# Where four small sets of products stand: openings, maxima and stores in a gated attention and MLP kernel

## The chip, the cores and the metric

The kernel runs on one core of one Trainium2 chip. The metric is the device time of one execution in microseconds (us). TensorE (PE in the profile, its weight loads PEld), VectorE (DVE), ScalarE (ACT), GpSimd (POOL) and SyncE (SP) run side by side; each works through its own instructions in the order in which the program issues them, and semaphores hold an instruction until the data that it needs are there.

## The reference

For a sequence of 2048 tokens of width 448, all in float32, the output is `g * a + (1 - g) * b`, where `g` is a sigmoid of a weighted sum of the token.

- `a` is attention: 16 heads of width 28 have their own queries and share one key and one value head; `softmax(q k / sqrt(28)) v`, then an output projection `wo`.
- `b` is a mixer: layernorm, `w1`, gelu, the four quarters of the channels shifted by +1, -1, +2 and -2 tokens, `w2`, added to x to give `x1`; then layernorm, `w3` (448 to 1792), gelu, `w4`, added to `x1`.

## The kernel before, in words

Most products are made in two parts for precision: an operand is split into a high part and the low rest (tiles ending in `h` and `l`), and three products take the place of one. Names of tiles in the profile come from the program, buffer numbers left out.

The order of every engine's instructions is the order of the program text (`manual_schedule`). There are three stages.

**Stage 1** makes queries, keys and values and the token mixing. It begins with 16 products of zeros on TensorE (L97 and L98), which need no loaded data. `first_queries` (L319) then makes the queries of token block 0 from the raw first chunk (L324) and the split chunks (L328). There are 16 query blocks `u`, four groups of heads (`g`) for each of four token blocks (`b`); `stage_q(u)` (L331) makes one with eleven products and `q_out` (L313) copies it out of PSUM and stores it to DRAM from ScalarE's queue (L317). The rows of keys and values ride in the same blocks; `stage_kv(b)` (L341) reads them back on SyncE's queue (L345, L348), and on the same queue come the first weights of stage 2 (L605). `ln1_send(b)` (L375) transposes the inverse standard deviations of token block b on TensorE, copies them on ScalarE and writes them to DRAM on SyncE; `ln1_read(b)` (L383) reads them back spread over the partitions (L386), for `stage_w1(b)`, whose VectorE step multiplies by them (L453). `split_w_high` runs on ScalarE and `split_w_low` on VectorE; `ln1_tile(b, t)` takes the statistics of one token tile on VectorE.

**Stage 2** is the MLP: for each of four token blocks a loop over 14 feature tiles f, `w3_part` (products L136 to L140, two gelus on ScalarE, a difference on VectorE) and, two tiles behind, `w4_part` for four token tiles (products L693 to L695). In the third and fourth token block `fill()` (L669) puts a job between the token tiles: four jobs make the score maxima of query block 0, one token tile each, and a fifth (`max_end`) puts them in place.

**What the maxima are.** So that exponentials don't overflow, a stand-in for the largest score of each query is taken over 16 keys only. `max_products` (L207) makes 16 small bf16 products for a query block, four for each token tile, one in each of four column tiles of the array; `max_reduce` (L215) reduces them on VectorE; `max_end` (L244) negates, splits and transposes the maxima and stores them on SyncE into spare rows of the query tile `qh`.

**Stage 3** is the attention: 128 cycles `c`, eight for each query block `u` (`u, i = divmod(c, 8)`). PSUM's eight banks are four `singles` and two `pairs`. A cycle handles two tiles of keys:

1. the first scores (24 products, L205) go into two singles `s0`, `s1` and into `pairs[0]`; ScalarE makes exponentials of the singles and VectorE copies the pair out (L929), so that the pair is soon free again;
2. the second scores go into the other two singles and `pairs[1]`; ScalarE makes their exponentials, and then those of the copied pair;
3. the values of the cycle before (L883) go into the bank of `s0` for the first half of the queries, and into that of `s1` for the second; `values_end` adds each to the output on VectorE (L805);
4. jobs, products of the output projection for the query block before (L831) with their add on VectorE (L847), stand between.

In the next cycle the singles change places: the second scores go where this cycle's `s0` and `s1` were. At `i == MAX_AT` (2), for the first 15 query blocks, the maxima of the next block are made as well: one job goes into `pairs[0]` between the two halves of the values, and the maxima's products go into the second half of `s0` behind them. In cycles without maxima the job goes into the second half of `s0`, and at `i == 2` of the last query block there are both jobs.

Of the kernel before, what the change touches and what calls it, by code (L numbers as in the profile page):

```python
# [42 lines left out]
def gated_mix_kernel(  # L43
# [50 lines left out]
        return psA.tile([P, 512], F32, tag="mx", bufs=1, name=name)  # L94

    wps = misc_tile("warm_ps")
    for _ in range(16):  # L97
        nc.tensor.matmul(wps[:, 0:256], warm[:, 0:P], warm, start=True, stop=True)  # L98

    def split_w_chunk(raw, wh, wl, c, cols=slice(None)):  # L100
# [9 lines left out]
    def split_w_high(raw, wh, wl):  # L110
        nc.scalar.copy(wh[:, 0:3, :], raw[:, 0:3, :])
        nc.gpsimd.memset(f32(wh)[64:128, 3, :], 0.0)
        nc.scalar.copy(wh[0:64, 3, :], raw[0:64, 3, :])
        nc.scalar.copy(wl[64:128, 3, :], raw[64:128, 3, :])

    def split_w_low(raw, wh, wl):
        for c in range(3):
            nc.vector.tensor_tensor(wl[:, c, :], raw[:, c, :], f32(wh)[:, c, :], ALU.subtract)
        nc.vector.tensor_tensor(wl[0:64, 3, :], raw[0:64, 3, :], f32(wh)[0:64, 3, :], ALU.subtract)
# [87 lines left out]
    def max_products(u, ts, ps):  # L207
        for i, t in enumerate(ts):
            for c in range(4):
                m = t * P + 32 * c  # L210
                q = f32(qh_of[u])[:, m:m + 32].bitcast(BF16).rearrange("p (m e) -> p m e", e=2)[:, :, 1]
                nc.tensor.matmul(ps[32 * c:32 * c + 32, i * 4 * MK:(i + 1) * 4 * MK], q, khd,
                                 start=True, stop=True, tile_position=(0, 32 * c))

    def max_reduce(u, ts, ps):  # L215
        if u not in mx_of:
            mx_of[u] = late.tile([P, 4, 4], F32, tag="mr", bufs=2, name=f"mr_{u}")
        n = len(ts)
        nc.vector.reduce_max(mx_of[u][:, :, ts[0]:ts[0] + n].rearrange("p j t -> p t j"),
                             ps[:, 0:n * 4 * MK].rearrange("p (t j k) -> p t j k", t=n, j=4), axis=AX.X)  # L220

    def max_part(u, ts, ps):
        max_products(u, ts, ps)
        max_reduce(u, ts, ps)
# [19 lines left out]
    def max_end(u):  # L244
        mr = mx_of.pop(u).rearrange("p j t -> p (j t)")
        mc = late.tile([P, 32], F32R, tag="mc", bufs=2, name=f"mc_{u}")
        nc.vector.tensor_scalar(mc[:, 0:16], mr, -1.0, None, op0=ALU.mult)
        nc.vector.scalar_tensor_tensor(mc[:, 16:32], mr, -1.0, f32(mc)[:, 0:16],
                                       op0=ALU.mult, op1=ALU.subtract)
        mrow = late.tile([P, 32], F32, tag="mrow", bufs=2, name=f"mrow_{u}")  # L250
        nc.vector.transpose(mrow, f32(mc))
        for k in range(2):
            rows = f32(qh_of[u])[DH + k:P:32, :].rearrange("j (t p q) -> p j t q", p=4, q=32)
            for p in range(4):
                nc.sync.dma_start(rows[p], mrow[32 * p + 16 * k:32 * p + 16 * k + 16, :])
# [4 lines left out]
    with tc.tile_pool(name="s1b", bufs=1) as s1b, \  # L260
# [52 lines left out]
        def q_out(u, ps):  # L313
            b, g = divmod(u, NG)
            qf = s1.tile([P, 512], F32, tag="qf", bufs=4, name=f"qf_{u}")
            nc.scalar.copy(qf, ps)
            nc.scalar.dma_start(qd[g, :, 512 * b:512 * b + 512], qf)  # L317

        def first_queries():  # L319
            ps = [mm1(f"q_{g}") for g in range(NG)]  # L320
# [10 lines left out]
        def stage_q(u, tile_of=mm1):  # L331
            b, g = divmod(u, NG)
            ps = tile_of(f"q_{u}")
            w = slice(g * P, (g + 1) * P)
            proj(ps, wqh[:, :, w], wql[:, :, w], *xact[b])
            q_out(u, ps)
# [31 lines left out]
        def ln1_tile(b, t):  # L368
            if t == 0:
                rs1_of[b] = stats_tiles(s1, b)  # L370
            stats_tile(s1, b, t, rs1_of[b][0])
            if t == 3:
                stats_end(*rs1_of[b])

        def ln1_send(b):  # L375
            ps = misc_tile(f"rsT_{b}")[0:4, 0:P]
            nc.tensor.transpose(ps, rs1_of.pop(b)[1], ident)
            rT = s1.tile([4, P], F32, tag="rT", bufs=2, name=f"rT_{b}")
            nc.scalar.copy(rT, ps)
            rb_of[b] = dram.tile([4, P], F32, tag="rsd", bufs=2, name=f"rsd_{b}")  # L380
            nc.sync.dma_start(rb_of[b], rT)
# [128 lines left out]
        centre_w1()  # L510
        stage_q(7)
        stage_q(8)
        ln1_send(0)
        ln1_read(0)
        split_w_high(w1raw, w1h, w1l)
        for t in range(4):
            ln1_tile(1, t)
        split_w_low(w1raw, w1h, w1l)
        stage_q(9)
        load_x(3)  # L520
        stage_q(10)
        load_x1(3)
# [137 lines left out]
    with tc.tile_pool(name="s2", bufs=1, reuse_waits="tile") as s2, \  # L660
# [2 lines left out]
            for n in range(n0, n1):  # L663
                nc.gpsimd.tensor_scalar(x1[:, n, :], x1[:, n, :], gi[:, n:n + 1], None, op0=ALU.mult)

        fills = [lambda t=t: max_part(0, (t,), (max_tile if t % 2 else misc_tile)(f"m_0_{t}")) for t in range(4)]
        fills += [lambda: max_end(0)]

        def fill():  # L669
            if fills:  # L670
# [85 lines left out]
    with tc.tile_pool(name="s3", bufs=1, reuse_waits="tile") as s3, \  # L756
# [38 lines left out]
        def values_end(u, pv, qs=slice(0, 512)):  # L795
            if u not in o_of:
                o_of[u] = s3.tile([P, 512], F32, tag="o", bufs=2, name=f"o_{u}")
                fresh.add(u)
            o = o_of[u][:, qs]
            if u in fresh:  # L800
                nc.vector.tensor_copy(o, pv)
                if qs.stop == 512:
                    fresh.remove(u)
            else:
                nc.vector.tensor_add(o, o, pv)  # L805
# [88 lines left out]
        def job_products(ps, n):  # L894
            adds = []
            for _ in range(min(n, len(jobs))):
                products, add, args, cols = jobs.pop(0)
                part = ps[:, 0:D // 2] if n == 1 else ps[:, cols]
                products(*args, part, cols)
                adds.append((add, args, part, cols))  # L900
            return adds
# [11 lines left out]
        for c in range(NC):  # L913
            u, i = divmod(c, NT // 2)
            k = 2 * c
            s0, s1, s2, s3_ = singles if c % 2 == 0 else singles[2:] + singles[:2]
            pa = score_tiles(u, 2 * i, s0, s1, pairs[0])
            with tc.block() if c in HINTS else nullcontext():
                if c in HINTS:
                    tc.mark_branch_hint_location("redo", "LikelyTaken", HINTS[c])  # L920
                exps(pa, left, s0.unsqueeze(1))
            exps(pa, right, s1.unsqueeze(1))
            if i == 2 and u == 0:
                q_begin(1)
            if i == 3 and u == 0:
                q_low(1)
                q_fetch(2)
            if c < NC - 1:
                nc.vector.tensor_copy(pa[:, both], pairs[0])  # L929
            else:  # L930
                exps(pa, both, pairs[0])
            if i == 4 and later:
                later.pop(0)()
            if i == 1 and sums:
                norms.append(recip(*sums.pop()))
            if i == 3 and norms:
                w = norms[0][0]
                norm(*norms.pop())
            if i == 5 and u + 2 < NU:
                q_begin(u + 2)  # L940
            if i == 6 and u + 2 < NU:
                q_low(u + 2)
                q_fetch(u + 3)
            pb = score_tiles(u, 2 * i + 1, s2, s3_, pairs[1])
            exps(pb, left, s2.unsqueeze(1))
            exps(pb, right, s3_.unsqueeze(1))
            exps(pb, both, pairs[1])
            if c < NC - 1:
                exps(pa, both)
            if u and i == (3 if u == NU - 1 else 4):  # L950
                jobs += [(wo_products, wo_add, (u - 1, t), cols) for t in range(4) for cols in halves]
            if c == 0:
                run_jobs(s0, 2)
                run_jobs(s1, 2)
                continue
            v = (c - 1) // (NT // 2)
            at_max = i == MAX_AT and u + 1 < NU
            q0, q1 = slice(0, 256), slice(256, 512)
            values((k - 2, k - 1), s0[:, q0], q0)
            values_end(v, s0[:, q0], q0)  # L960
            if i == MAX_AT:
                run_jobs(pairs[0][:, 0], 1)
            values((k - 2, k - 1), s1[:, q0], q1)
            if at_max:
                max_products(u + 1, range(4), s0[:, q1])
                values_end(v, s1[:, q0], q1)
                max_reduce(u + 1, range(4), s0[:, q1])
                later.append(lambda u=u: max_end(u + 1))
            else:
                adds = job_products(s0[:, q1], 1)  # L970
                values_end(v, s1[:, q0], q1)
                job_adds(adds)
            if i == 0 and v < NU - 1:
                sums.append(sums_begin(v))
        assert not sums and not norms and not later and len(jobs) == 3
# [143 lines left out]
```

## Time and profile before

| | us |
|---|---|
| median of 3 runs | 928.12 |
| the runs | 927.07, 928.12, 928.72 |
| the profiled execution, its own time | 929.3 |
| its span | 927.4 |

The span runs from the first to the last instruction that the profile shows. In a row of a timeline stand the start and the length in us, the engine, the line of the kernel, the operation, and the tiles as `out<-in` with their shapes; `x16` merges neighbours of one kind, and the length then runs from the first start to the last end; in brackets stand the engine's idle time before it and who ended it. A busy length of a matmul includes its drain, so neighbours overlap, and the distance between starts tells the pace. In a row of waits stand the sum in us, the number of waits and the longest. "issue" means that nothing in the profile shows what was waited for.

### The profile page before, as it was taken

Reading aid. Unit: us, or ns where it says so; the run is one execution under the profiler, and the core shown is the slowest. Engines: PE = TensorE matmul, PEld = TensorE weight load, DVE = VectorE, ACT = ScalarE, POOL = GpSimd, SP = SyncE. Lnnn points to the kernel's source line nnn. Section 1 sums busy time; section 2 is a strip of 40 time slices with the busy share of each in tenths; the row PEclk is TensorE's granted clock in tenths of the full one; section 3 lists DMA queues with packets and bytes.
Section 4 is the critical chain, followed back from the end, with each engine's and each line's share of the span. In section 5 each row is a group of like instructions: output and inputs, shape, how many; then the busy total and the mean of one; then the engine's idle time right before and its main releaser. Section 6 shows DMA issues by size and latency. Waiting matters only on the chain.

```text
span 927.4 us, 24251 instructions
## 1 busy us (share of the span) xinstructions
PE 913.3 (98%) x10348; PEld 627.8 (68%) x10348; DVE 519.3 (56%) x965; ACT 636.0 (69%) x1002; POOL 80.3 (9%) x116
## 2 busy tenths in 40 slices
PE   9999999999999999999999999999999999999997
PEld 6788888888888888875555555555555555555553
DVE  3665273631431431146666776777667767766664
ACT  5542345322222132169999999999999999999994
POOL 3243320200000520020000000000000000000000
PEclk9999999999999999999999999999999999999999
DMA  9822643120110110010000001000011000010001
GB/s 309 296 66 55 183 131 126 39 66 1 40 46 2 33 53 1 1 51 23 17 22 21 16 20 49 23 25 15 25 33 39 20 24 14 25 44 13 14 14 43
DMA packets 40584, 47.32 MB, mean 51 GB/s; under 512 B 10137, under 2 KB 28633, under 8 KB 40473
## 3 DMA queue, kind: packets, MB, share of 16 engines
q1 hardware_dynamic: 37160, 40.04, 14.7%
q10 hardware_dynamic: 3312, 5.70, 1.7%
q8 instruction: 82, 1.34, 0.6%
q14 instruction: 30, 0.24, 0.1%
HBM read 32.56 MB, written 11.67 MB: 48 GB/s over the span
## 4 chain that ended last, share of the span: by engine, by line
PE 94%; ACT 4%; issue 1%; DVE 1%; DMA 1%; DVEq 0%; ACTq 0%
PE bank L883 25%; PE bank L205 18%; PE bank L831 5%; PE acc L693 5%; PE acc L695 5%; PE acc L694 5%; PE g L137 4%; PE g L138 4%; PE g L136 4%; ACT p L872 4%; PE pair L205 2%; PE hs L471 1%; PE hs L472 1%; PE g L140 1%; PE g L139 1%; PE h L136 1%
## 5 line engine op out<-in xcount | busy, mean ns | idle before, releaser
L872 ACT ACTIVATE p<-bank 128x512 f32<-128x512 f32 x512 | 265.5, 611 | 11.1 <-POOL ones L857 4.2
L883 PE MATMUL bank<-p,vext 128*32 128x256 f32 x4064 | 248.4, 382 | 5.7 <-ACT p L872 2.0
L883 PEld LDWEIGHTS bank<-p,vext 128*32 128x32 f32 x4064 | 119.0, 109 | 124.4 <-ACT p L872 59.8
L929 DVE COPY p<-pair 128x1024 f32<-128x1024 f32 x127 | 155.6, 1225 | 54.9 <-PE pair L205 40.1
L683 ACT ACTIVATE gh<-g 128x512 fp32r<-128x512 f32 x55 | 32.9, 599 | 187.3 <-PE g L140 187.3
L805 DVE TENSOR_TENSOR o<-o,bank 128x256 f32<-128x256 f32 x222 | 93.5, 421 | 90.1 <-PE bank L883 73.9
L872 ACT ACTIVATE p<-p 128x1024 f32<-128x1024 f32 x127 | 139.8, 1101 | 0.0
L872 ACT ACTIVATE p<-pair 128x1024 f32<-128x1024 f32 x129 | 137.3, 1064 | 0.0
L685 DVE TENSOR_TENSOR gl<-gf,gh 128x512 fp32r<-128x512 f32 x55 | 38.2, 694 | 168.6 <-ACT gf L684 168.6
L205 PE MATMUL bank<-qh,kh 32*128 32x512 f32 x512 | 116.4, 448 | 0.1
L205 PE MATMUL pair<-qh,kh 32*128 32x512 f32 x512 | 116.1, 449 | 0.3 <-DVE x L750 0.3
L205 PE MATMUL bank<-qh,kl 32*128 32x512 f32 x512 | 102.1, 390 | 0.0
L205 PE MATMUL pair<-qh,kl 32*128 32x512 f32 x512 | 101.5, 390 | 0.0
L205 PE MATMUL bank<-ql,kh 32*128 32x512 f32 x512 | 101.3, 388 | 0.0
L205 PE MATMUL pair<-ql,kh 32*128 32x512 f32 x512 | 100.7, 388 | 0.0
L205 PEld LDWEIGHTS bank<-qh,kh 32*128 32x128 f32 x512 | 48.1, 181 | 60.7 <-issue 34.3
L693 PE MATMUL acc<-w4h,gh 128*128 128x448 f32 x220 | 80.6, 366 | 0.0
L695 PE MATMUL acc<-w4h,gl 128*128 128x448 f32 x220 | 80.4, 366 | 0.0
L694 PE MATMUL acc<-w4l,gh 128*128 128x448 f32 x220 | 80.2, 364 | 0.0
L137 PE MATMUL g<-al,w3h 128*128 128x512 f32 x168 | 65.9, 393 | 0.0
L138 PE MATMUL g<-ah,w3l 128*128 128x512 f32 x168 | 65.9, 392 | 0.0
L136 PE MATMUL g<-ah,w3h 128*128 128x512 f32 x168 | 65.8, 392 | 0.0
(210 smaller groups left out, 1402.1 us busy)
## 6 DMA issues: line engine op xcount, KB each, us to landing
qd<-qf ACTq DMA_DIRECT2D x16, 256.0 KB
rb<-rd SPq DMA_DIRECT2D x15, 256.0 KB
x<-in_x_dram SPq DMA_DIRECT2D x4, 896.0 KB
xd<-xt SPq DMA_DIRECT2D x16, 224.0 KB
w34raw<-in_w_dram SPq DMA_DIRECT2D x7, 512.0 KB
qr<-qd SPq DMA_DIRECT2D x64, 56.0 KB
w34raw<-in_w_dram SPq DMA_DIRECT2D x7, 448.0 KB
out_dram<-ot SPq DMA_DIRECT2D x14, 224.0 KB
```

What stands on the lines that cost most here:

```text
L136: nc.tensor.matmul(ps, wh[:, c, :], ah[:, c, :], start=(c == 0), stop=False)
L137: nc.tensor.matmul(ps, wh[:, c, :], al[:, c, :], start=False, stop=False)
L138: nc.tensor.matmul(ps, wl[:, c, :], ah[:, c, :], start=False, stop=False)
L205: nc.tensor.matmul(ps[j], k[h, keys], q[h, :], start=(r == 0), stop=(r == 2), tile_position=(32 * j, 0))
L693: nc.tensor.matmul(ps, gh[:, tok], w4h[i][:, k, :], start=(f == 0), stop=False)
L694: nc.tensor.matmul(ps, gh[:, tok], w4l[i][:, k, :], start=False, stop=False)
L695: nc.tensor.matmul(ps, gl[:, tok], w4h[i][:, k, :], start=False, stop=(f == stop))
L805: nc.vector.tensor_add(o, o, pv)
L831: nc.tensor.matmul(ps[32 * i:32 * i + 32, :], a[:, c:c + 32], w, start=start, stop=stop, tile_position=(0, 32 * i))
L872: nc.scalar.activation(p[:, heads], p[:, heads] if source is None else source, AF.Exp, scale=SCALE)
L883: nc.tensor.matmul(pv[32 * j:32 * j + 32, :], vext[:, kt, :], p_of[k][:, j, qs], start=(k == ks[0]), stop=(k == ks[-1]), tile_position=(0, ...
L929: nc.vector.tensor_copy(pa[:, both], pairs[0])
```

## The change

There are five edits, all of order or place; what is computed is the same.

- Twenty products of zeros at the start in place of 16.
- The store of the last query block (`u == 15`) is issued by SyncE, not by ScalarE.
- In stage 1, behind query block 8: first the split of `w1` and the statistics of token block 1, then query block 9, and only then the sending and reading of token block 0's inverse deviations.
- The maxima of query block 0 are one fill of 16 products and one reduction, in one bank, and `max_end` is the second fill.
- In the cycles with maxima, their products and the reduction come between the two halves of the values, in `pairs[0]`; the job comes behind the second half, in the second half of `s0`, as in all other cycles.

```diff
     wps = misc_tile("warm_ps")
-    for _ in range(16):
+    for _ in range(20):
         nc.tensor.matmul(wps[:, 0:256], warm[:, 0:P], warm, start=True, stop=True)
...
             nc.scalar.copy(qf, ps)
-            nc.scalar.dma_start(qd[g, :, 512 * b:512 * b + 512], qf)
+            (nc.sync if u == NU - 1 else nc.scalar).dma_start(qd[g, :, 512 * b:512 * b + 512], qf)
...
         stage_q(8)
+        split_w_high(w1raw, w1h, w1l)
+        split_w_low(w1raw, w1h, w1l)
+        for t in range(4):
+            ln1_tile(1, t)
+        stage_q(9)
         ln1_send(0)
         ln1_read(0)
-        split_w_high(w1raw, w1h, w1l)
-        for t in range(4):
-            ln1_tile(1, t)
-        split_w_low(w1raw, w1h, w1l)
-        stage_q(9)
         load_x(3)
...
-        fills = [lambda t=t: max_part(0, (t,), (max_tile if t % 2 else misc_tile)(f"m_0_{t}")) for t in range(4)]
-        fills += [lambda: max_end(0)]
+        fills = [lambda: max_part(0, range(4), misc_tile("m_0")), lambda: max_end(0)]
...
             values_end(v, s0[:, q0], q0)
-            if i == MAX_AT:
+            if at_max:
+                max_part(u + 1, range(4), pairs[0][:, 0])
+                later.append(lambda u=u: max_end(u + 1))
+            elif i == MAX_AT:
                 run_jobs(pairs[0][:, 0], 1)
             values((k - 2, k - 1), s1[:, q0], q1)
-            if at_max:
-                max_products(u + 1, range(4), s0[:, q1])
-                values_end(v, s1[:, q0], q1)
-                max_reduce(u + 1, range(4), s0[:, q1])
-                later.append(lambda u=u: max_end(u + 1))
-            else:
-                adds = job_products(s0[:, q1], 1)
-                values_end(v, s1[:, q0], q1)
-                job_adds(adds)
+            adds = job_products(s0[:, q1], 1)
+            values_end(v, s1[:, q0], q1)
+            job_adds(adds)
```

`max_part` calls `max_products` and then `max_reduce`.

## The prediction

> **What bounds the kernel now.** I read the page first: engine shares and the chain that ended last.
>
> ```profile
> PE 913.3 (98%) x10348; PEld 627.8 (68%) x10348; DVE 519.3 (56%) x965; ACT 636.0 (69%) x1002; POOL 80.3 (9%) x116
> PE 94%; ACT 4%; issue 1%; DVE 1%; DMA 1%; DVEq 0%; ACTq 0%
> ```
>
> TensorE is busy for 98% of the span and carries 94% of the chain. So I ask of each edit one thing: does TensorE get through its instructions sooner or later at that place, and does something behind it hold the difference back? Three places matter: the opening (0 to 11 us), the four fills in the third pass of the MLP (274 to 282 us), and 15 cycles of the attention loop.
>
> The opening, first TensorE's timeline, then its waits up to 375 us, then its weight loads:
>
> ```profile
> 1.05 3.59 PE L98 MATMUL warm_ps<-warm 128*128 128x256 bf16 x16 [1.05 <-DVE warm L66]
> ```
> ```profile
> PE q L324 <- DMA wqraw<-in_wq_dram: 0.8, 1, 0.8
> ```
> ```profile
> 5.41 0.50 PEld L324 LDWEIGHTS q<-xkv,wqraw 128*128 128x128 f32 x2 [1.25 <-DMA wqraw<-in_wq_dram]
> 6.43 0.33 PEld L324 LDWEIGHTS q<-xkv,wqraw 128*128 128x128 f32 x1 [0.52 <-issue]
> ...
> 8.99 0.33 PEld L324 LDWEIGHTS q<-xkv,wqraw 128*128 128x128 f32 x1 [0.52 <-issue]
> 9.83 0.19 PEld L324 LDWEIGHTS q<-xkv,wqraw 128*128 128x128 f32 x1 [0.50 <-issue]
> 10.26 0.19 PEld L324 LDWEIGHTS q<-xkv,wqraw 128*128 128x128 f32 x1 [0.24 <-issue]
> 10.69 0.19 PEld L328 LDWEIGHTS q<-ahk,wqh 128*128 128x128 f32 x1 [0.24 <-issue]
> ```
>
> The 16 products of zeros end at 4.64; TensorE then waits 0.8 us for the query weights. From 5.41 the loads of L324 come 0.85 us apart (6.43 to 8.99 in three steps), and from 9.83 they come 0.43 apart: the same work at twice the pace, 4.4 us after the break ended. Apart from the start at L98, this is the only wait of TensorE's products before 375 us. Time won here therefore reaches the end, if the data keep ahead.
>
> **The change part by part. 1, the opening.** Four more products at 3.59 / 16 = 0.22 us end at about 5.5, so the break is filled and L324 starts up to 0.12 late. Eight slow and fast steps last 10.69 - 5.41 = 5.28 us; eight at the fast pace would last 3.44. The trace doesn't show an unbroken opening, so I bound it: at worst the pace changes when it did, and the edit loses 0.12; at best all eight are fast, a gain of 1.84 - 0.12 = 1.7. If 4.4 us of unbroken work bring the pace, they are over at 1.05 + 4.4 = 5.45, when L324 begins. I take 1.6, near the upper end.
>
> [...]
>
> **2, the fills.** Rows of one of the four, in TensorE's timeline:
>
> ```profile
> 279.66 0.36 PE L694 MATMUL acc<-w4l,gh 128*128 128x448 f32 x1
> 279.86 0.37 PE L695 MATMUL acc<-w4h,gl 128*128 128x448 f32 x1
> 280.16 0.21 PE L212 MATMUL m<-khd,qh 128*32 128x64 bf16 x4
> 280.30 0.47 PE L693 MATMUL acc<-w4h,gh 128*128 128x448 f32 x1
> 280.61 0.36 PE L694 MATMUL acc<-w4l,gh 128*128 128x448 f32 x1
> ```
>
> Undisturbed, these products follow each other by 0.20 (279.66 to 279.86). From L695 (279.86) to the second product behind the fill (280.61) it is 0.75 in place of 0.41, so each fill costs 0.34, mostly the change of tile shape in and out. Four cost 1.36. In one piece the change is paid once, and three more rounds of four products follow. A round costs about 0.03: the loop's 16 products with all that follows take 0.23 (574.28 to 574.51 below). So one piece costs 0.34 + 0.09 = 0.43, and 0.9 is saved. Bounds: 0.3 if every round cost 0.2 more, 1.0 if rounds were free. On VectorE, busy for 56% of the span, four small reductions become one; the maxima's end comes two feature tiles earlier, with its small stores on SyncE, and is needed only by the attention loop, over a pass of the MLP later. If that cover were gone, the loop's first scores would wait.
>
> [...]
>
> **3, the loop.** A normal cycle and one with maxima, in TensorE's, ScalarE's and VectorE's timelines:
>
> ```profile
> 568.20 1.93 PE L883 MATMUL bank<-p,vext 128*32 128x256 f32 x32
> 569.95 0.56 PE L831 MATMUL bank<-wof,on 128*32 128x224 f32 x8
> 570.45 0.50 PE L205 MATMUL bank<-qh,kh 32*128 32x512 f32 x2
> ...
> 571.25 0.39 PE L205 MATMUL bank<-qh,kh 32*128 32x512 f32 x2
> ...
> 572.15 1.07 PE L883 MATMUL bank<-p,vext 128*32 128x256 f32 x16
> 573.04 0.56 PE L831 MATMUL pair<-wof,on 128*32 128x224 f32 x8
> 573.42 1.05 PE L883 MATMUL bank<-p,vext 128*32 128x256 f32 x16
> 574.28 0.30 PE L212 MATMUL bank<-khd,qh 128*32 128x64 bf16 x16
> 574.51 0.50 PE L205 MATMUL bank<-qh,kh 32*128 32x512 f32 x2
> ...
> 575.40 0.50 PE L205 MATMUL bank<-qh,kh 32*128 32x512 f32 x2
> ...
> 576.30 1.07 PE L883 MATMUL bank<-p,vext 128*32 128x256 f32 x16
> ```
> ```profile
> 570.38 1.09 ACT L872 ACTIVATE p<-p 128x1024 f32<-128x1024 f32 x1
> 571.50 2.06 ACT L872 ACTIVATE p<-bank 128x512 f32<-128x512 f32 x4
> ...
> 574.33 1.09 ACT L872 ACTIVATE p<-p 128x1024 f32<-128x1024 f32 x1
> 575.57 1.08 ACT L872 ACTIVATE p<-bank 128x512 f32<-128x512 f32 x2
> ```
> ```profile
> 571.52 1.23 DVE L929 COPY p<-pair 128x1024 f32<-128x1024 f32 x1 [0.46 <-PE pair L205]
> 573.35 0.42 DVE L805 TENSOR_TENSOR o<-o,bank 128x256 f32<-128x256 f32 x1 [0.60 <-PE bank L883]
> 573.69 0.45 DVE L847 SCALAR_TENSOR_TENSOR ot<-pair,gg,ot 128x224 f32<-128x224 f32 x1
> 574.59 0.42 DVE L805 TENSOR_TENSOR o<-o,bank 128x256 f32<-128x256 f32 x1 [0.46 <-ACT p L872]
> 574.93 0.42 DVE L219 TENSOR_REDUCE mr<-bank 128x16 f32<-128x256 f32 x1
> ```
> ```profile
> PEld bank L205 <- DVE mr L219: 5.3, 15, 0.4
> ```
>
> A cycle is a ring: the first scores (570.45) let ScalarE begin (571.50), its first exponential frees the bank for the values (572.15), and values and job stand ahead of the next first scores (574.51). A normal cycle lasts 572.15 - 568.20 = 3.95; the one with maxima lasts 576.30 - 572.15 = 4.15. ScalarE itself is hardly idle (570.38 + 1.09 = 571.47, next start 571.50), so a ring can't shrink much below 3.95.
>
> The 0.20 has two parts. From the values to the next first scores it is 2.36 (572.15 to 574.51) against 2.25 (568.20 to 570.45): 0.11 for the maxima's products. And the second scores come 0.89 behind the first (574.51 to 575.40) against 0.80 (570.45 to 571.25), because they need the bank that the reduction reads until 574.93 + 0.42 = 575.35. All 15 cycles have this wait. It makes the values start 0.73 behind ScalarE (575.57 to 576.30) in place of 0.65 (571.50 to 572.15).
>
> Now the new order. Products of the maxima take the job's place at 573.04 and last about 0.11; the second half of the values follows and its job last: 0.89 + 0.11 + 0.86 + 0.50 (a job ahead of scores, 569.95 to 570.45) = 2.36, as before. Nothing is won or lost on the first scores, if weights of the values load behind the maxima without a pause; the nearest rows for a pause are those of the fill, 0.11 into and 0.11 behind L693, so 0 to 0.22, and I take 0, since here both sides are column tiles and the step into the maxima (573.42 to 574.28, four rounds of 0.215) shows none. The reduction runs at 573.77 to 574.19, behind the first output half, and the pair that it reads is free 0.3 ahead of the scores. The second output half is there at about 574.2 (0.26 earlier than from 573.42 on, since the maxima are shorter than the job), and VectorE adds it and then the job, 0.42 + 0.45, until about 575.1, as the bank in a normal cycle is free 0.6 behind the first scores. So the second scores come at about 575.3 and the 0.08 goes: 15 x 0.08 = 1.2. What is late next is ScalarE's first exponential, as in a normal cycle.
>
> **4, the moves.** The sending of the first inverse deviations goes behind query block 9 and the split of w1 ahead of it; the last query store goes to SyncE. Rows of SyncE, VectorE, SyncE and ScalarE:
>
> ```profile
> 35.34 0.33 SPq L386 DMA_DIRECT2D rsb<-rsd  x1
> ```
> ```profile
> 42.01 0.69 DVE L453 TENSOR_TENSOR hf<-h,rsb 112x512 f32<-112x512 f32 x1 [0.32 <-PE h L140]
> ```
> ```profile
> 103.38 0.61 SPq L605 DMA_DIRECT2D w34raw<-in_w_dram  x1
> ```
> ```profile
> 115.82 0.83 ACT L111 CAST w3h<-w34raw 128x768 fp32r<-128x768 f32 x1
> ```
>
> The sending moves behind eleven products of about 0.2, so the read would go out at about 37.5 in place of 35.34 (35.9 with the opening's gain), and with it on SyncE the loads of the fourth token block; the first use is at 42.01, or 40.4, so it has 3 us or more to land. If that were missed, VectorE waits first: four banks are there for the stage's four products, and TensorE would stop only after a whole stage. In exchange the split of w1, which that stage loads as weights, is ready earlier. The store on SyncE waits there for ScalarE's copy, and the key and value reads queued behind it wait too; that pushes the load at 103.38 by about an issue (0.61), and its data aren't used until 115.82. I cost all of it at nothing; the cover is 3 us in the one case and over 8 in the other, less the load's own time.
>
> **Sum.** 1.6 + 0.9 + 1.2 = 3.7 us. Against the profiled execution: 929.3 (span 927.4, 1.9 around it) becomes 925.6. That execution lies 1.2 above the median of 928.12, so the forecast in those terms is 924.4.
>
> **The rivals.** (a) *The zeros don't bring the pace.* Nothing shows that they count as work; the 4.4 us may begin only at L324. Then 0.1 is lost in place of 1.6 won: 926.1. (b) *The date of the pace differs from run to run.* The three runs differ by 1.65 us (927.07 to 928.72); if that is the old opening at half pace for some 3 us more or less, a run without the break can win another 1.5: 922.9. [...] That the profiled execution lies above all three runs speaks against a still later date in them. (c) *The maxima in the middle cost as at a fill*: 0.22 - 0.08 = 0.14 more in 15 cycles, a loss of 2.1 in place of 1.2 won: 927.7. (d) *Slower: the pair is held.* Should the reduction run only behind the second output half, as at 574.93 in the old order, the first scores, which now need the pair, wait until 575.35 in place of 574.51: 15 x (0.84 - 0.08) = 11.4 lost, 937.0. It decides once the reduction ends after 574.51, 0.3 later than worked out; the diff issues it ahead of that output half, which speaks against. (e) *Nothing comes of it*: (a) and (c) together leave 0.9 - 0.1 - 2.1, some 929.4.
>
> **How the numbers follow.** Forecast 0.54, (a) 0.14, (b) 0.09, (c) 0.12, (e) 0.06, (d) 0.05. The forecast's own spread is 923.3 to 925.6. A measurement can tell about 0.2% (1.9 us) from no change, so faster means under 926.26. Faster: the forecast and (b), half of (a), and a third of (c), whose 0.22 is an upper end: 0.74. Same: the rest of (a) and (c) and two thirds of (e): 0.19. Slower: (d) and a third of (e): 0.07. The range leaves out (d), (e), and the outer parts of (b) and (c): 922.8 to 927.3.
>
> **What would show it.** [...] In the fills L212 stands once with x16 and costs 0.4. The wait of the second scores on the reduction is gone, and a cycle with maxima is followed by one of 3.95. Wrong would be a first score later than 2.36 behind the values, a wait of L205 on L219, or a new wait of TensorE before 375 us.

## The result, and the profile after

| | before | after |
|---|---|---|
| median of 10 runs each, us | 928.63 | 925.38 |
| lowest to highest, us | 927.07 to 931.87 | 924.82 to 926.83 |
| span of the profiled execution, us | 927.4 | 923.5 |

The ratio is 0.9963, 95% interval 0.9954 to 0.9973: 0.37% faster, or 3.3 us by the medians. The forecast was 3.7 (924.4 from 928.12). In the profiled executions the difference of the spans is 3.9.

Where it came from can be read by dating the same instruction in both traces. The opening first: TensorE's weight loads in the changed kernel.

```profile
1.04 3.97 PEld L98 LDWEIGHTS <-warm 128*128 128x128 bf16 x20 [1.04 <-DVE warm L66]
5.26 0.30 PEld L324 LDWEIGHTS q<-xkv,wqraw 128*128 128x128 f32 x2 [0.25 <-DMA wqraw<-in_wq_dram]
5.80 0.19 PEld L324 LDWEIGHTS q<-xkv,wqraw 128*128 128x128 f32 x1 [0.24 <-issue]
6.23 0.19 PEld L324 LDWEIGHTS q<-xkv,wqraw 128*128 128x128 f32 x1 [0.24 <-issue]
...
8.37 0.19 PEld L328 LDWEIGHTS q<-ahk,wqh 128*128 128x128 f32 x1 [0.24 <-issue]
```

The loads stand 0.43 us apart from the second on, and L328 is reached at 8.37 instead of 10.69: 2.3 us sooner. TensorE's waits up to 375 us, in the changed kernel, are one row:

```profile
PE warm_ps L98 <- DVE warm L66: 1.0, 1, 1.0
```

No new wait stands behind the opening, so the 2.3 us are still there when the MLP begins (its first product stands at 124.89 against 127.23). Then the fill, in TensorE's timeline (line numbers from here on are one lower than before):

```profile
271.87 0.37 PE L694 MATMUL acc<-w4h,gl 128*128 128x448 f32 x1
272.17 0.30 PE L212 MATMUL m<-khd,qh 128*32 128x64 bf16 x16
272.40 0.47 PE L692 MATMUL acc<-w4h,gh 128*128 128x448 f32 x1
272.71 0.36 PE L693 MATMUL acc<-w4l,gh 128*128 128x448 f32 x1
```

From the product ahead of the fill to the second one behind it are 0.84 us (271.87 to 272.71), 0.43 more than undisturbed. Last, a cycle with maxima and the next one: TensorE, VectorE, ScalarE.

```profile
568.79 1.07 PE L882 MATMUL bank<-p,vext 128*32 128x256 f32 x16
569.68 0.30 PE L212 MATMUL pair<-khd,qh 128*32 128x64 bf16 x16
569.80 1.05 PE L882 MATMUL bank<-p,vext 128*32 128x256 f32 x16
570.66 0.56 PE L830 MATMUL bank<-wof,on 128*32 128x224 f32 x8
571.16 0.50 PE L205 MATMUL bank<-qh,kh 32*128 32x512 f32 x2
...
571.95 0.39 PE L205 MATMUL bank<-qh,kh 32*128 32x512 f32 x2
```
```profile
569.99 0.42 DVE L804 TENSOR_TENSOR o<-o,bank 128x256 f32<-128x256 f32 x1 [0.60 <-PE bank L882]
570.33 0.42 DVE L219 TENSOR_REDUCE mr<-pair 128x16 f32<-128x256 f32 x1
570.97 0.42 DVE L804 TENSOR_TENSOR o<-o,bank 128x256 f32<-128x256 f32 x1 [0.22 <-issue]
571.31 0.45 DVE L846 SCALAR_TENSOR_TENSOR ot<-bank,gg,ot 128x224 f32<-128x224 f32 x1
```
```profile
568.14 2.06 ACT L871 ACTIVATE p<-bank 128x512 f32<-128x512 f32 x4 [0.28 <-PE pair L205]
...
572.21 2.07 ACT L871 ACTIVATE p<-bank 128x512 f32<-128x512 f32 x4
...
576.16 2.06 ACT L871 ACTIVATE p<-bank 128x512 f32<-128x512 f32 x4
```

The maxima take 0.12 between the two halves of the values, the first scores come 2.37 behind the values as in the old order, and the second scores 0.79 behind the first. By ScalarE's starts the cycle with maxima lasts 4.07 (568.14 to 572.21) and the next one 3.95 (572.21 to 576.16); it had been 4.03 (575.57 to 579.60). The wait of L205 on L219 is gone from the list of waits.

The first exponential of the loop stands at 402.75 against 406.08, that of its last cycle at 906.30 against 910.26. So the loop wins 0.6 us in this pair of traces, less than its cycles with maxima say, because each trace has a few long cycles of its own at other places.

### The profile page after: what moved, and what is told of

Same layout as the page of the kernel before. It is cut to its first block, busy times and chain, and to the rows that moved or that the text cites. A ratio compares the mean times of both kernels' runs of the same rounds, so it can differ in the third digit from the quotient of the medians.

```text
span 923.5 us, 24257 instructions
## 1 busy us (share of the span) xinstructions
PE 909.3 (98%) x10352; PEld 625.6 (68%) x10352; DVE 519.2 (56%) x962; ACT 635.5 (69%) x1002; POOL 79.4 (9%) x116
## 4 chain that ended last, share of the span: by engine, by line
PE 93%; ACT 4%; issue 1%; DVE 1%; DMA 0%; DVEq 0%; ACTq 0%
PE bank L882 25%; PE bank L205 17%; PE bank L830 6%; PE acc L694 5%; PE acc L692 5%; PE acc L693 5%; PE g L137 4%; ACT p L871 4%; PE g L138 4%; PE g L136 4%; PE pair L205 2%; PE hs L471 1%; PE hs L472 1%; PE g L140 1%; PE g L139 1%; PE h L136 1%
## 5 line engine op out<-in xcount | busy, mean ns | idle before, releaser
L205 PE MATMUL pair<-qh,kh 32*128 32x512 f32 x512 | 114.5, 442 | 0.3 <-DVE x L749 0.3
L205 PE MATMUL bank<-qh,kh 32*128 32x512 f32 x512 | 114.7, 442 | 0.0
L205 PE MATMUL bank<-qh,kl 32*128 32x512 f32 x512 | 101.9, 390 | 0.0
L205 PE MATMUL pair<-qh,kl 32*128 32x512 f32 x512 | 101.6, 390 | 0.0
L205 PE MATMUL bank<-ql,kh 32*128 32x512 f32 x512 | 101.1, 388 | 0.0
L205 PE MATMUL pair<-ql,kh 32*128 32x512 f32 x512 | 100.8, 388 | 0.0
L205 PEld LDWEIGHTS bank<-qh,kh 32*128 32x128 f32 x512 | 48.2, 181 | 61.2 <-issue 36.5
L830 PE MATMUL bank<-wof,on 128*32 128x224 f32 (+1 forms) x976 | 69.6, 359 | 0.6 <-DVE o L804 0.3
```

The lines of the kernel that those rows point to most:

```text
L205: nc.tensor.matmul(ps[j], k[h, keys], q[h, :], start=(r == 0), stop=(r == 2), tile_position=(32 * j, 0))
L830: nc.tensor.matmul(ps[32 * i:32 * i + 32, :], a[:, c:c + 32], w, start=start, stop=stop, tile_position=(0, 32 * i))
```

## The experiments

Three sets: each part alone on the kernel before; four variants of the changed kernel, one that holds the reduction back and three with another opening; and each part undone in the changed kernel. Ratios are to the kernel before, on the same chip, with 95% intervals. Where a median is set against the changed kernel's 925.38, the two may come from different chips, between which the kernel before differs by up to 0.6 us; the ratios don't have this. Since single parts are worth about 0.1%, the traces carry the verdicts and the timings confirm or limit them.

### The opening alone

```diff
-    for _ in range(16):
+    for _ in range(20):
```

> The kernel before with 20 products of zeros, nothing else changed. Theory (unbroken work brings the fast pace): L324's loads stand 0.43 us apart from the first on, L328 starts at about 8.4 instead of 10.7, and the 2.3 us reach the end: 0.9975 of the kernel before. Rival (the zeros don't count, the changed kernel's profile was a lucky date): the pace changes at 8.8 us or later, 1.000. Rival (the gain needs the moves of the changed kernel to be carried through): L328 early, but a wait of TensorE before 50 us, 0.999 to 1.000.

Measured: 0.9987 (0.9978 to 0.9996). In the profile L328's load comes at 8.67, and no wait of TensorE follows. The third expectation, that the gain wouldn't be carried through, falls in this execution. But the timing shows only 1.2 us of the 2.0 that this profile has, and the 0.9975 of the theory lies just outside the interval. The next runs give two reasons: the old opening isn't always slow, and a quick one can lose at a later place.

### The loop alone

The kernel before with the last hunk of the change only.

> The kernel before with the new order in the loop alone. Theory: the wait of the second scores on the reduction goes, the cycle behind one with maxima falls from 4.03 to 3.95 by ScalarE's starts, the cycle with maxima stays at 4.07; 14 or 15 times 0.08 is 1.1 to 1.2 us, 0.9988. Rival (the maxima in the middle cost a pause of the weight loads): 4.07 rises to 4.1 or more, 0.999 to 1.002.

Measured: 1.0003 (0.9993 to 1.0013), which is none of the gain. The trace tells three things. First, the old opening of 16 products was quick here as well:

```profile
5.42 0.30 PEld L324 LDWEIGHTS q<-xkv,wqraw 128*128 128x128 f32 x2 [1.25 <-DMA wqraw<-in_wq_dram]
5.95 0.19 PEld L324 LDWEIGHTS q<-xkv,wqraw 128*128 128x128 f32 x1 [0.24 <-issue]
...
8.53 0.19 PEld L328 LDWEIGHTS q<-ahk,wqh 128*128 128x128 f32 x1 [0.24 <-ACT ahk L127]
```

The same break of about 1 us stands ahead of 5.42, and yet the fast pace is there at once. The break doesn't always cost. (It is 0.77 us by TensorE's waits, and 1.0 if the drain of the last product isn't counted.) Second, half of what the quick opening won was lost again in stage 1, at the transpose that the change moves (TensorE, then VectorE):

```profile
30.73 0.27 PE L377 MATMUL rsT<-ident,rs_s 128*4 128x128 f32 x1 [1.07 <-DVE w1raw L401]
```
```profile
28.38 2.21 DVE L401 SCALAR_TENSOR_TENSOR w1raw<-wsum_ps,w1raw 128x448 f32<-128x448 f32 x4
```

The transpose writes the one `misc` bank, which VectorE still reads for the sum of `w1` until 28.38 + 2.21 = 30.59. TensorE, ahead of time, waits 1.07 us. Third, in the loop the cycles behind those with maxima are 3.94 or 3.95 long, as expected, but six others, those with `i == 1` of every second query block from 2 to 12, end late, because ScalarE starts the next one late:

```profile
471.20 2.07 ACT L872 ACTIVATE p<-bank 128x512 f32<-128x512 f32 x4
...
475.42 1.09 ACT L872 ACTIVATE p<-bank 128x512 f32<-128x512 f32 x2 [0.30 <-PE pair L205]
```

Such a cycle lasts 4.22 in place of 3.95, though the scores that it names ended 0.3 us earlier. Six times 0.28 is 1.7 us, more than the loop's 1.1: from the first cycle's start to the last one's this loop lasts 504.1 us, as in the kernel before (504.2). Dated against the first scores, ScalarE starts 1.33 us behind them at these six places and 1.05 in a normal cycle. Of the other profiles three have one such start (the kernel before at 858.38, the opening alone, the fill alone) and the rest none; their other long cycles have late scores. In three of the four that the changed kernel has, VectorE waits ahead of them for a small DMA (0.34 us at 565.52, 0.29 at 605.44, 0.55 at 827.83). Why this profile has six in step was not settled, nor whether the executions without a profile have them.

### The fill alone

```diff
-        fills = [lambda t=t: max_part(0, (t,), (max_tile if t % 2 else misc_tile)(f"m_0_{t}")) for t in range(4)]
-        fills += [lambda: max_end(0)]
+        fills = [lambda: max_part(0, range(4), misc_tile("m_0")), lambda: max_end(0)]
```

> The kernel before with one fill of 16 products in place of four. Theory: one change of tile shape in place of four, the third pass of the MLP is 0.95 us shorter, 0.9990. [...] An opening at another date can move the single profile by 2 us in either direction, so the pass is to be read by itself.

Measured: 0.9994 (0.9985 to 1.0004). The third pass of the MLP, from the first product of its first tile to that of the next pass, took 69.97 us (264.09 to 334.06) against 70.94 before: 0.97 less. That is the theory's size; in the timing, the interval holds both the theory's 0.9990 and no change.

### The moves alone

```diff
         stage_q(8)
+        split_w_high(w1raw, w1h, w1l)
+        split_w_low(w1raw, w1h, w1l)
+        for t in range(4):
+            ln1_tile(1, t)
+        stage_q(9)
         ln1_send(0)
         ln1_read(0)
-        split_w_high(w1raw, w1h, w1l)
...
-            nc.scalar.dma_start(qd[g, :, 512 * b:512 * b + 512], qf)
+            (nc.sync if u == NU - 1 else nc.scalar).dma_start(qd[g, :, 512 * b:512 * b + 512], qf)
```

> The kernel before with the sending of the inverse deviations behind query block 9, the split of w1 ahead of it, and the last query store on SyncE. Theory: all of it is hidden, no wait of TensorE, 1.000 within 0.0005. Rival: the later loads of the fourth token block hold stage 1, 0.5 us or more longer; or it wins 0.5 us where ScalarE held TensorE.

Measured: 0.9993 (0.9982 to 1.0004): not told from no change. The opening was quick in this profile (8.58 for L328), and no wait of TensorE follows it: the transpose stands at 32.07, behind query block 9.

### The reduction held back

The changed kernel, with the reduction behind the addition of the second output half.

```diff
-                max_part(u + 1, range(4), pairs[0][:, 0])
+                max_products(u + 1, range(4), pairs[0][:, 0])
...
             values_end(v, s1[:, q0], q1)
+            if at_max:
+                max_reduce(u + 1, range(4), pairs[0][:, 0])
             job_adds(adds)
```

> The changed kernel with the reduction issued behind the addition of the second output half, still from the pair. Theory: the next first scores need the pair and wait until the reduction ends, about 0.8 us later than without, in 15 cycles: 10 to 12 us slower than the changed kernel, about 1.008 of the kernel before. Rival (the ring has slack there, or the two products for the singles go ahead): under 3 us slower than the changed kernel, 1.000 or less.

Measured: 1.0044 (1.0028 to 1.0061), 932.88 us, 7.5 over the changed kernel's median: between the two expectations. The list of TensorE's waits has the row that the prediction feared, here on the pair:

```profile
PEld pair L205 <- DVE mr L219: 7.0, 15, 0.8
```

And in the timeline, TensorE and VectorE:

```profile
573.88 0.50 PE L205 MATMUL bank<-qh,kh 32*128 32x512 f32 x2
574.50 0.50 PE L205 MATMUL pair<-qh,kh 32*128 32x512 f32 x2
```
```profile
574.03 0.42 DVE L219 TENSOR_REDUCE mr<-pair 128x16 f32<-128x256 f32 x1
```

The scores for the singles start, those for the pair wait 0.62 us for the reduction's end. The cycle with maxima becomes 4.48 long (ScalarE's starts at 570.86 and 575.34), the next one 4.05: 0.41 and 0.10 more than in the changed kernel, 14 x 0.51 = 7.1 us. (The cycle of query block 1 adds another 0.7.) So the rival was real and its place right; against the changed kernel the price was put at 0.84 a cycle and is 0.51.

### Forty products

```diff
-    for _ in range(20):
+    for _ in range(40):
```

> The changed kernel with 40 products of zeros. Theory (a fixed stretch of unbroken work brings the pace): the products' distance falls from 0.213 to 0.107 us at about 5.2 us, they end at about 7.4, and L324 starts 2.1 us later than with 20: the end is 2.1 us later, 0.9985 of the kernel before. [...] Rival (zeros don't count): it doesn't change among the zeros at all, they end at 9.6, 1.001.

Measured: 0.9979 (0.997 to 0.9988), 926.74 us, 1.4 over the changed kernel. The pace changes among the zeros: the 40 loads take 6.46 us, where 20 took 3.97, so the later ones run at the double pace.

```profile
1.05 6.46 PEld L98 LDWEIGHTS <-warm 128*128 128x128 bf16 x40 [1.05 <-DVE warm L66]
7.51 0.30 PEld L324 LDWEIGHTS q<-xkv,wqraw 128*128 128x128 f32 x2
```

The trace also keeps a record of the clock that was granted to TensorE. Its full part begins at 5.58: 22 products start before it, 0.213 us apart, and 18 after it, 0.109 apart. The date lies near the 5.2 of the theory. L324 is 2.25 us later than in the changed kernel, and the first products of the MLP still are (127.16 against 124.89); in the loop some of it is hidden, since this profile has fewer long cycles (502.9 us from the first start to the last, against 503.6).

### A later start of the zeros

```diff
-    nc.vector.memset(warm, 0.0)
...
+    nc.vector.memset(x1[:, 0:4, :], 0.0)
+    nc.vector.memset(warm, 0.0)
```

> The changed kernel with a memset of 1792 elements of x1 on VectorE ahead of the one that the zeros need, so that the 20 products start 1 to 2 us later. Theory (a stretch of about 4.2 us from the first product on): the pace changes 4.2 us behind the first product, at 6.2 to 7.2, and L324 starts 0.9 to 1.9 us late. [...]

Measured: 0.9982 (0.9973 to 0.9991). The products begin 1.9 us later, and the pace changes 2.8 us behind the first, not 4.2:

```profile
2.92 3.43 PEld L99 LDWEIGHTS <-warm 128*128 128x128 bf16 x20 [2.92 <-DVE warm L70]
6.36 0.30 PEld L325 LDWEIGHTS q<-xkv,wqraw 128*128 128x128 f32 x2
```

Twenty loads in 3.43 in place of 3.97 are five distances halved; the clock record has the change at 5.73. A fixed stretch of 4.2 us behind the first product is thereby out, and the date is not fixed to the start of the program either (it was 5.21 in the changed kernel).

### Eighteen products

```diff
-    for _ in range(20):
+    for _ in range(18):
```

> The changed kernel with 18 products of zeros: they end at about 4.9, a break of 0.4 us before L324. Theory (any break starts the count again): the pace comes at 9 us or later, 2.3 us slower than the changed kernel, 0.9988 of the kernel before. Rival (a short break is forgiven): the pace comes at about 5.2, as fast as the changed kernel, 0.9963.

Measured: 0.997 (0.9961 to 0.998), 925.62 us: not told from the changed kernel. The first product of L324 was slow, the others fast (the clock turned full at 5.96), and L328 came at 8.78. A break of half a microsecond (0.4 by the list of waits) was forgiven.

### The loop undone

The changed kernel with the old order in the loop.

> The changed kernel with the old order in the loop. Theory (the loop's gain was given back in the run of the loop alone by late starts of ScalarE that belong to that build's layout): the cycles behind those with maxima return to 4.03, 1.1 us slower than the changed kernel, 0.9976 of the kernel before if the changed one is at 0.9963 to 0.997. Rival (the new order makes no difference to the time of a run): as fast as the changed kernel.

Measured: 0.9974 (0.9963 to 0.9984), 926.71 us. The old wait is back, 15 times, and the cycles behind those with maxima are 4.03 long again, 14 of them 0.08 or 0.09 over the others.

```profile
PEld bank L205 <- DVE mr L219: 5.3, 15, 0.4
```

By medians it is 1.3 us slower than the changed kernel, but the intervals overlap. The traces are finer: from the first cycle's start to the last one's, the loop lasts 503.9 to 504.9 us in the five profiles with the old order (504.35 in the mean) and 502.7 to 503.6 in the seven with the new one that have no other change in the loop (503.25), the run of the loop alone left out. So the loop is worth its 1.1 us, and what hid it in the profile of the loop alone were the late starts of ScalarE.

### The sending undone

The changed kernel with `ln1_send(0)` and `ln1_read(0)` back ahead of the split of `w1`, and that split in its old order.

> The changed kernel with the sending of the inverse deviations back in front of query block 9 and ahead of the split of w1 (the store stays on SyncE). Theory: with the early opening TensorE reaches the transpose before VectorE has read the bank that it shares with the sum of w1; TensorE waits 0.5 to 1.1 us at L377 and the end is as much later, 0.997 to 0.998 of the kernel before. Rival (the moves are hidden, as predicted): no wait, as fast as the changed kernel.

Measured: 0.997 (0.9958 to 0.9982), 926.6 us: 1.2 over the changed kernel by medians, but the intervals overlap, and the cost is not told from the timing. In the profile TensorE waits at the transpose, though briefly, because here the pace came only at 7.01:

```profile
30.60 0.27 PE L377 MATMUL rsT<-ident,rs_s 128*4 128x128 f32 x1 [0.17 <-DVE w1raw L401]
```

### The opening undone

```diff
-    for _ in range(20):
+    for _ in range(16):
```

> The changed kernel with 16 products of zeros. [...] Rival (the break always costs): 2.3 us slower, 0.9988. Rival (the profile of the kernel before was a rare case): as fast as the changed kernel.

Measured: 0.9975 (0.9964 to 0.9986), 927.61 us. The eleven runs fall into groups: 925.24, 925.30, 925.94 and 925.96, then 926.78, then 927.61, 927.65, 927.82, 927.90, 927.99 and 928.04. The profiled one is of the slow group (the clock turned full at 10.43); its loads:

```profile
9.81 0.34 PEld L324 LDWEIGHTS q<-xkv,wqraw 128*128 128x128 f32 x1 [0.52 <-issue]
10.56 0.19 PEld L324 LDWEIGHTS q<-xkv,wqraw 128*128 128x128 f32 x1 [0.41 <-issue]
10.99 0.19 PEld L328 LDWEIGHTS q<-ahk,wqh 128*128 128x128 f32 x1 [0.24 <-issue]
```

The upper group lies about 2.2 us above the lower one, about as much as between L328 at 10.99 and at 8.5 or 8.8. With 16 products the opening loses this in about half of the executions (six or seven of these eleven, two of the five profiles with 16 products); with 20 in none that was profiled, only up to 0.9 (L328 at 9.28 in the run above).

### The fill undone

The changed kernel with four fills.

> The changed kernel with four fills. Theory: the third pass of the MLP is 0.95 us longer, and so is the run, 0.001 more than the changed kernel's ratio. Rival: the gain of the pass is lost before the end, as fast as the changed kernel.

Measured: 0.9966 (0.9952 to 0.998), 925.94 us. The third pass is 70.94 us long (264.13 to 335.07) against 69.97 in the changed kernel (263.97 to 333.94): 0.97 again. The timing, 0.6 over the changed kernel's median, is too coarse to add to that.

## Why the prediction was right, point by point

**What bounds.** Right: TensorE's place in its order carried every gain to the end, and the list of its waits up to 375 us got no new row.

**1, the opening: 1.6 forecast, 2.3 between the two profiles, 0.6 to 2.2 in the runs.** With the break filled the pace came sooner, as argued (L328 at 8.37 in place of 10.69), and rival (a) is out, since with forty products the pace changes among the zeros (40 loads in 6.46 us, 20 in 3.97). Three things in the working were off. The upper end of 1.7 was too low: the pace was there before L324, L324 began 0.15 earlier rather than 0.12 later, as the weights landed sooner, and the eight distances took 3.1, not 3.44 (the first of them is short, as in the old rows, where two loads stand in the first 1.02 us). The 4.4 us of unbroken work, counted as a fixed stretch, are out: of two profiles that start 20 products at 1.05, the clock turned full at 5.21 in this one and at 7.01 in that of the sending undone. And the one profile was taken for the rule, while rival (b), "the date of the pace differs from run to run", was given 0.09 and worked out only towards a larger gain. The profile of before was a bad draw: the old opening got its pace early in about half of the executions, so the median gains less than the pair of traces shows (by the ratios 1.2 with the opening alone and 1.1 with the opening undone; by the medians 0.6 and 2.2). That 1.6 lies between these and the 2.3 of the pair is luck. What sets the date was not shown. A break of half a microsecond passed (L328 at 8.78 with eighteen products); one of a microsecond passed in some executions (8.50, 8.53 and 8.58) and not in others (10.69, 10.99).

**2, the fills: 0.9 forecast, 0.97 measured.** One piece costs 0.43 as worked out. Its sixteen products start within 0.11 us, 7 ns apart in the mean (272.170 to 272.277). The 0.97 was read twice, with the fill alone and with it undone.

**3, the loop: 1.2 forecast, 1.1 measured.** 0.12 for the maxima, 2.37 to the first scores, 0.79 to the second, 3.95 for the next cycle: each as worked out, in 14 cycles rather than 15, since the ring of query block 1 runs differently. Rival (c), a pause of the weight loads, did not occur. Rival (d) didn't either. It was overpriced: with the values moved up, the held reduction ends 0.57 behind the first scores (574.45 against 573.88) and not 0.84 (575.35 against 574.51), so that its old place, read from the old rows, was no longer its place in the new order; and the scores for the singles go ahead of it.

**4, the moves: nothing forecast.** The size held: the moves alone are not told from no change, and no profile with the new order has a new wait of TensorE before 375 us. Both reasons for it were off. First, the cover of 3 us for the read was not there. In the changed kernel ScalarE copies the transpose out only behind the split of `w1`, 4.1 us after it (35.91 against 31.84); the read goes out at 38.06, though the opening is early, and VectorE waits for it:

```profile
42.37 0.69 DVE L453 TENSOR_TENSOR hf<-h,rsb 112x512 f32<-112x512 f32 x1 [2.81 <-DMA rsb<-rsd]
```

Eight of the nine profiles with the new order name this DMA there, after 2.0 to 3.2 us of VectorE's idle time. What hides it is the second cover that the prediction named, the four banks: TensorE makes all four products of the stage meanwhile and begins those of the next token block at 47.26, when the first bank has long been free. Second, the old order can cost. Four profiles have it with an early pace. In two of them TensorE waits at the transpose, 1.07 us (the loop alone) and 0.17 (the sending undone), for a PSUM bank that VectorE still reads; in the other two (the opening alone, the fill alone) it doesn't. In the opening alone (TensorE, then VectorE) the read ends at 27.08 + 2.20 = 29.28, ahead of the transpose:

```profile
29.67 0.27 PE L377 MATMUL rsT<-ident,rs_s 128*4 128x128 f32 x1
```
```profile
27.08 2.20 DVE L401 SCALAR_TENSOR_TENSOR w1raw<-wsum_ps,w1raw 128x448 f32<-128x448 f32 x4
```

What differs is ScalarE's cast of a later chunk (L127), behind which VectorE's work on that chunk, its statistics and this read follow. It starts at 19.69 and 19.87 in the two without the wait and at 21.03 and 21.17 in the two with it, where ScalarE waits for the chunk's DMA. So an early TensorE and a late chunk together make the wait. The prediction looked at who waits for the moved step and not at which bank the step itself waits for once TensorE is ahead. In the changed kernel's own execution VectorE ended that read at 27.97 + 2.21 = 30.18, by the row

```profile
27.97 2.21 DVE L401 SCALAR_TENSOR_TENSOR w1raw<-wsum_ps,w1raw 128x448 f32<-128x448 f32 x4
```

and the transpose, at 31.84 in the new order, would have stood one query block of 2.5 us earlier, at 29.3: by this estimate some 0.8 us would have been lost there. How often the moves win this was not measured, and moving the store alone was not tried.

**Sum.** 3.7 forecast, 3.3 measured: about 1.2 from the opening together with the moves that can keep it, 0.97 from the fill, 1.1 from the loop. Undone one at a time, the opening, the fill, the loop and the sending raise the ratio by 0.0012, 0.0003, 0.0011 and 0.0007, together 0.0033 of the 0.0037; each of these has an interval as wide as itself or wider, so the shares rest on the traces.

## What to carry to other kernels

When one engine carries the whole chain, a gain early in it is kept only if the engine, now ahead of time, finds its banks and operands free: follow each wait of its order with the new dates. A difference that shows in one pair of traces can be a draw; date the same event in several executions before it is counted in full. And where a buffer is shared, put the reader in the queue ahead of work that can wait, and price the rival order with the new dates, not the old ones.

## What was not expected of the hardware

- The same opening got its fast pace at different dates. With 20 products from 1.05 on, L328's load stands at 8.37, 8.49, 8.53, 8.54, 8.67 and 9.28 in the six profiles that have it. With 16 products it stands at 8.50, 8.53 and 8.58 in three profiles and at 10.69 and 10.99 in two.
- The break doesn't tell these two groups of the 16 products apart: TensorE's weight loads stood idle ahead of L324 for 1.2 or 1.3 us in each of the five. What does was not settled.
- The trace's record of the granted clock has its full part from 9.80 on in the kernel before and from 5.21 on in the changed one. PEclk in the profile's views counts the time ahead of it as full: it is 1.00 from 5 to 9 us in the kernel before, where the loads of L324 stand 0.85 us apart.
- ScalarE now and then begins an exponential 0.28 us later than a normal cycle would have it, with nothing in the profile that it waits for. In one profile this happened in every sixteenth cycle, six times, and cost 1.7 us, as much as a real improvement; three of the other profiles have it once, ten not at all. What it is stays open.
